# Two chunks of attention scores to a PSUM bank, and one mask matmul for both

## The chip, the cores and the metric

The kernel runs on one core of one Trainium2 chip. The metric is the device time of one execution in microseconds (us), lower is better. A time given for a kernel is the median of its runs; the profile is one execution of its own, taken by the hardware profiler.

## What is computed

Causal attention with a bias from a running sum, and behind it two feed-forward stages. The change lies in the attention alone (B = 4, H = 8, S = 576, D = 64):

```python
scores = scale * np.matmul(q, k.transpose(0, 1, 3, 2))
causal = np.triu(np.ones((S, S), dtype=bool), k=1)
cum = np.cumsum(np.maximum(s, 0.0), axis=-1)
bias = -(cum[:, :, :, None] - cum[:, :, None, :])
scores = np.where(causal, -1000000000.0, scores + np.minimum(bias, 0.0))
attn = np.exp(scores - np.max(scores, axis=-1, keepdims=True))
attn = attn / (np.sum(attn, axis=-1, keepdims=True) + 1e-09)
out = np.matmul(attn, v)
...
h = x @ w_in; g = h - np.tanh(h); x = g @ w_out        # 2304 x 512, width 2048
# then: each token through one of 8 experts, picked by argmax, width 1024
```

## The kernel before

**Tiling.** Two heads at a time fill the 128 partitions, which gives 16 pairs of heads, called heads below where no harm is done. The 576 queries of a pair are cut into nine chunks of 64; chunk c needs the first 64c + 64 keys. `score(c)` (lines 216 to 235) multiplies chunk c with those keys into a tile `sc`, one PSUM bank of 128 x 512 floats. It takes three matmuls on line 228, since each operand is split into a high and a low part. A fourth matmul (line 230) adds the causal mask to the last 64 columns: it multiplies the identity `identb` with `maskm`, a 128 x 64 block in bf16. Chunk 8 has 576 keys and takes two banks. One VectorE operation (line 233, called the reduction below) then adds the bias that waits in `P`, scales, writes the result to `P` and leaves the least value of each row in `m`. `expo(c)` (line 238) takes the exponential on ScalarE, with `m` as its bias and the sum of each row to `den`.

**What follows.** `ptr(g)` (line 253) transposes four blocks of `P` at a time into a tile `tp`; its copy to SBUF (line 135) is on VectorE for groups 0, 2 and 4 and on ScalarE for the others. `pv` (line 272) multiplies with V, and line 280 scales the result by the inverse of `den`, which makes a trip through DRAM in between (lines 292 to 323). GpSimd writes the bias (line 209) and makes the low parts of K and Q (line 181), from copies that ScalarE casts (lines 190 and 198). Beside this the weights of the next stage are converted on ScalarE and VectorE (lines 382 to 386).

**PSUM.** The eight banks are given out as rings: three for `tp`, four for `sc`, one for `pv`. A pair asks for ten `sc` banks. A bank is free again when its reduction is done.

**Order.** Each step has a place in time, a number in the table `AT`; pair number i adds 9 i to it, so that one unit is one chunk. The steps are written out in the order of these numbers. For pair i, `score(8 - n)` stands at n and its `expo` at n + 0.8; group 5 of the transposes at 5.5, group 3 at 6.5, group 4 at 7.5, group 1 at 8.5; the cast of a later pair's K falls at 8.5 as well. TensorE runs exactly in this order (`ORD[MA]`). The other engines are ordered by a planner, which starts from the same sequence and may move an instruction whose inputs are there earlier; `behind()` ties some steps, among them the conversion of weights on VectorE, to the last reduction written out before them (`k.mark["D"]`), or on ScalarE to the last exponential (`k.mark["A"]`).

Of the kernel before, what the change touches and what calls it, by code (L numbers as in the profile page):

```python
# [8 lines left out]
F32 = mybir.dt.float32  # L9
# [4 lines left out]
ALU = mybir.AluOpType  # L14
PSUM = bass.MemoryType.PSUM

B, H, S, D = 4, 8, 576, 64
# [21 lines left out]
def setup_attention(ctx, tc, k, s):  # L39
# [47 lines left out]

    k.qb = [[k.e1.tile([128, NCH, 128], F32R, name=f"qb{i}_{t}", tag=f"qb{i}_{t}", bufs=1) for t in range(2)] for i in range(NQB)]
    for i, q in enumerate(k.qb):
# [8 lines left out]
    for p in k.P:  # L98
# [4 lines left out]
NCH = 9  # L103
PW = [0, 128, 256, 512, 768, 1152, 1536, 2048, 2560, 3200]

BLK = [(kc, c) for kc in range(5) for c in range(2 * kc, NCH)]
NQB = 3

EV = {0: 'D', 1: 'A', 2: 'D', 3: 'A', 4: 'D', 5: 'A', 6: 'A'}
PIN = 'D1'  # L110
# [4 lines left out]
AT = {'ni': 14, 'no': 2, 'pad': 60.5, 'const': 42.5, 'wl': 6.2, 'cr': -9.0, 'load': -20.0, 'v': 6.0, 'ks': -9.5, 'qs': -8.5,  # L115
# [22 lines left out]
def attention_events(tc, k, q, kk, v, xT, b, hp, idx):  # L138

    nc = tc.nc  # L140
    bh = b * H + 2 * hp
    ld, wk, ps = k.ld, k.wk, k.psum
    ev = []
    T = {}
    P = k.P[idx % 2]
    qh, ql = k.qb[idx % NQB]

    def at(t):
        def deco(f):
            ev.append((9 * idx + t, f))  # L150
            return f
        return deco
# [48 lines left out]
    def chunk(c, lo=0, hi=None):  # L201
        return P[:, PW[c] + lo:PW[c] + (64 * c + 64 if hi is None else hi)]

    def bias(c):

        w = 64 * c + 64
        ci = k.cumi[:, c, bh // 2:bh // 2 + 1]
        if BIAS[c] == "P" and (idx or c % 2):
            ins = nc.gpsimd.tensor_scalar(chunk(c), T["cr"][:, 0:w], 1.0, ci, ALU.mult, ALU.add)  # L209
            behind(tc, k, "P", ins)  # L210
            k.mark["P"] = ins.ins.name
        else:
            nc.vector.tensor_scalar(chunk(c), T["cr"][:, 0:w], ci, None, ALU.add)


    def score(c):
        if c == NCH - 1:
            T["m"] = wk.tile([128, NCH], F32, name="m", tag="m")
            T["m2"] = wk.tile([128, 1], F32, name="m2", tag="m2")
            T["den"] = wk.tile([128, NCH], F32, name="den", tag="den")  # L220
        w = 64 * c + 64
        least = 3.0e38
        cuts = [0, 288, 576] if w > 512 else [0, w]
        for lo, hi in zip(cuts, cuts[1:]):
            sc = ps.tile([128, 512], F32, name="sc", tag="sc")
            n = hi - lo
            for i, (a, x) in enumerate(((qh, "kh"), (qh, "kl"), (ql, "kh"))):
                nc.tensor.matmul(sc[:, 0:n], a[:, c, :], T[x][:, lo:hi], start=(i == 0), stop=(i == 2 and hi < w))  # L228
            if hi == w:
                nc.tensor.matmul(sc[:, n - 64:n], k.identb, k.maskm, start=False, stop=True)  # L230
            dst = chunk(c, lo, hi)
            m = T["m"][:, c:c + 1] if hi == w else T["m2"]
            k.mark["D"] = nc.vector.tensor_tensor_reduce(  # L233
                out=dst, in0=sc[:, 0:n], in1=dst, scale=-0.125, scalar=least, op0=ALU.add, op1=ALU.min, accum_out=m).ins.name
            least = m

    def expo(c):
        k.mark["A"] = nc.scalar.activation(  # L238
            chunk(c), chunk(c), AF.Exp, bias=T["m"][:, c:c + 1], scale=-1.0, accum_out=T["den"][:, c:c + 1]).ins.name

    for n in range(NCH):
        at(n + AT["bias"] - (4 if idx == 0 and n % 2 else 0))(lambda c=NCH - 1 - n: bias(c))
        at(n)(lambda c=NCH - 1 - n: score(c))
        at(n + AT["exp"])(lambda c=NCH - 1 - n: expo(c))


    def ptr(g):
# [731 lines left out]
def tile_kernel(ctx, tc, q, kk, v, s, w_in, w_out, w_gate, w_og, w1, w2, out, dbg=None):  # L979
# [7 lines left out]
    with ExitStack() as abctx:  # L987
# [3 lines left out]
        with ExitStack() as actx:  # L991
# [14 lines left out]
            for i in range(16):  # L1006
                ev += attention_events(tc, k, q, kk, v, xT, i // 4, i % 4, i)
# [81 lines left out]
```

## Time and profile before

| | |
|---|---|
| median of 3 runs | 945.45 us |
| lowest and highest run | 936.3 and 946.69 us |
| the profiled execution | 940.23 us, its span 938.6 us |
| granted TensorE clock, mean of the span | 0.990 |
| busy, share of the span | PE 95%, PEld 81%, DVE 66%, ACT 57%, POOL 39% |
| attention | about the first 200 us of the span |

PE is TensorE's matmuls, PEld its weight loads (they overlap), DVE is VectorE, ACT ScalarE, POOL GpSimd, SP SyncE. Ends of matmuls are modelled and overlap the next one, so a matmul's cost is read from its start to the start of the next one, not from its length. An execution's own time is 1.6 us above its span.

### The profile page before, as it was taken

What the parts mean: (1) busy time and instruction counts of PE and PEld (TensorE: products, weight loads), DVE (VectorE), ACT (ScalarE), POOL (GpSimd) and SP (SyncE); (2) the same over time, 40 slices, a digit from 0 to 9 for tenths busy, and PEclk for the clock granted to TensorE, in tenths of its full rate; (3) what the DMA queues carried; (4) which work ended last, traced back from release to release, by engine and by line L of the source; (5) the groups of instructions that cost most, each with busy time, mean ns of one, the idle gap of its engine ahead of it and who ended that gap; (6) DMA issues with size and microseconds to landing.
All of it is one profiled execution on the core that took longest, in us unless ns stands there. A gap on an engine that the chain in (4) does not pass through costs nothing.

```text
span 938.6 us, 16275 instructions
## 1 busy us (share of the span) xinstructions
PE 895.0 (95%) x5840; PEld 764.0 (81%) x5841; DVE 618.3 (66%) x1343; ACT 536.2 (57%) x1092; POOL 361.5 (39%) x396
## 2 busy tenths in 40 slices
PE   7999999988999989999999999999899999999995
PEld 5777777767887778888989898988788888888884
DVE  7888888959898887786555555577535444445420
ACT  6888888846666558455555555566344444444421
POOL 8888888714444432333323232323221220220111
PEclk9999999989999999999999999999989999999998
DMA  6666666581221121000000000232565555564100
GB/s 207 187 196 202 201 202 199 171 274 46 68 68 47 66 68 64 5 1 24 1 23 1 23 1 24 84 121 88 132 226 166 179 163 166 164 191 142 50 24 29
DMA packets 41362, 100.82 MB, mean 107 GB/s; under 512 B 9313, under 2 KB 9445, under 8 KB 41277
## 3 DMA queue, kind: packets, MB, share of 16 engines
q1 hardware_dynamic: 37117, 89.51, 31.1%
q0 software_dynamic: 4160, 10.23, 3.1%
q8 instruction: 47, 0.77, 0.4%
q14 instruction: 38, 0.31, 0.1%
HBM read 84.74 MB, written 15.79 MB: 107 GB/s over the span
## 4 chain that ended last, share of the span: by engine, by line
PE 64%; DVE 15%; issue 9%; ACT 6%; DMA 4%; POOL 1%; SPq 0%; DVEq 0%; POOLq 0%; ACTq 0%
PE h L577 14%; PE x L607 12%; PE y L844 11%; PE hc L820 10%; PE sc L228 6%; PE pv L272 4%; PE tp L253 4%; DVE d L589 3%; DVE t L591 3%; DVE d L587 2%; DVE wt L385 1%; DVE wt L386 1%; ACT u L584 1%; ACT t L586 1%; ACT P L238 1%
## 5 line engine op out<-in xcount | busy, mean ns | idle before, releaser
L577 PE MATMUL h<-x_h,wi 128*128 128x256 f32 x1152 | 221.4, 285 | 3.3 <-DVE t L590 3.3
L594 POOL TENSOR_TENSOR gl<-t,gh 128x512 fp32r<-128x512 f32 x72 | 100.4, 1394 | 262.9 <-ACT gh L593 176.1
L577 PEld LDWEIGHTS h<-x_h,wi 128*128 128x128 f32 x1152 | 183.8, 191 | 11.2 <-PE x L607 6.4
L607 PE MATMUL x<-wo,gh 128*128 128x512 f32 x576 | 180.0, 393 | 0.3 <-POOL wo L525 0.3
L577 PE MATMUL h<-x_l,wi 128*128 128x256 f32 x576 | 162.8, 283 | 0.0
L607 PE MATMUL x<-wo,gl 128*128 128x512 f32 x288 | 115.0, 399 | 8.8 <-POOL gl L594 8.7
L587 DVE TENSOR_TENSOR d<-u,h 128x512 f32<-128x512 f32 x72 | 49.3, 685 | 105.7 <-ACT t L586 105.6
L607 PEld LDWEIGHTS x<-wo,gh 128*128 128x128 f32 x576 | 103.6, 189 | 18.7 <-POOL wo L525 0.7
L577 PEld LDWEIGHTS h<-x_l,wi 128*128 128x128 f32 x576 | 110.1, 191 | 1.3
L228 PE MATMUL sc<-kh,qb 128*128 128x288 f32 (+8 forms) x320 | 101.6, 347 | 0.7 <-DVE m L233 0.7
L238 ACT ACTIVATE P<-P,m 128x576 f32<-128x576 f32 (+2 forms) x144 | 81.2, 565 | 31.5 <-DVE m L233 30.5
L807 DVE SCALAR_TENSOR_TENSOR gl<-hc,gh 128x336 fp32r<-128x336 f32 (+2 forms) x66 | 32.8, 497 | 91.7 <-ACT gh L806 91.7
L593 ACT CAST gh<-t 128x512 fp32r<-128x512 f32 x72 | 44.7, 621 | 83.9 <-DVE t L591 60.9
L806 ACT ACTIVATE gh<-hc 128x336 fp32r<-128x336 f32 (+2 forms) x66 | 29.2, 443 | 95.8 <-PE hc L820 83.9
L820 PE MATMUL hc<-xgh,w_h 128*128 128x336 f32 (+1 forms) x256 | 82.1, 321 | 0.0
L742 DVE TENSOR_TENSOR w_l<-w_r,w_h 128x1024 fp32r<-128x1024 f32 (+1 forms) x72 | 79.5, 1113 | 3.1 <-PE h L577 2.7
L820 PE MATMUL hc<-xgh,w_l 128*128 128x336 f32 (+1 forms) x256 | 79.9, 312 | 0.0
L820 PE MATMUL hc<-xgl,w_h 128*128 128x336 f32 (+1 forms) x256 | 79.7, 311 | 0.0
L209 POOL TENSOR_SCALAR P<-cr,cumi 128x448 f32<-128x448 f32 (+4 forms) x139 | 78.1, 579 | 1.9 <-ACT cr L135 0.4
L607 PEld LDWEIGHTS x<-wo,gl 128*128 128x128 f32 x288 | 54.1, 188 | 28.0 <-POOL gl L594 16.7
L844 PE MATMUL y<-w_h,gh 128*128 128x512 f32 (+1 forms) x192 | 76.1, 397 | 0.0
L844 PE MATMUL y<-w_l,gh 128*128 128x512 f32 (+1 forms) x192 | 76.0, 396 | 0.0
(192 smaller groups left out, 1962.4 us busy)
## 6 DMA issues: line engine op xcount, KB each, us to landing
w_r<-in_moe_w_dram SPq DMA_DIRECT2D x64, 512.0 KB, 3.6
f64raw<-in_moe_w_in_dram SPq DMA_DIRECT2D x16, 512.0 KB, 4.4
f64raw<-in_moe_w_out_dram SPq DMA_DIRECT2D x16, 512.0 KB, 4.1
vt<-in_v_dram SPq DMA_DIRECT2D x16, 320.0 KB, 5.1
xk<-in_k_dram SPq DMA_DIRECT2D x16, 288.0 KB, 2.8
xq<-in_q_dram SPq DMA_DIRECT2D x16, 288.0 KB, 3.4
x_d<-x2s SPq DMA_DIRECT2D x9, 512.0 KB, 2.8
cr<-cum_d SPq DMA_DIRECT2D x30, 144.0 KB, 4.4
```

The costliest lines, as they stand in the source:

```text
L209: ins = nc.gpsimd.tensor_scalar(chunk(c), T["cr"][:, 0:w], 1.0, ci, ALU.mult, ALU.add)
L228: nc.tensor.matmul(sc[:, 0:n], a[:, c, :], T[x][:, lo:hi], start=(i == 0), stop=(i == 2 and hi < w))
L238: k.mark["A"] = nc.scalar.activation(chunk(c), chunk(c), AF.Exp, bias=T["m"][:, c:c + 1], scale=-1.0, accum_out=T["den"][:, c:c + 1]).ins.name
L253: nc.tensor.transpose(pt[:, 128 * i:128 * i + 128], chunk(c, 128 * kc, 128 * kc + 128), k.ident)
L577: nc.tensor.matmul(ps[:, i, :], a[f][:, c, :], x[:, c, :], start=(n == 0), stop=(n == 11))
L587: nc.vector.tensor_tensor(d, u, ps, ALU.mult)
L593: nc.scalar.copy(gh, t)
L594: k.mark["P"] = nc.gpsimd.tensor_tensor(gl, t, gh.bitcast(F32), ALU.subtract).ins.name
L607: nc.tensor.matmul(st["x2", g][t], a[:, i, 128 * t:128 * t + 128], w[f], start=(f == 0 and n == 0), stop=(f == 15 and n == 2),)
L742: pin(tc, "1D"[e > 0], nc.vector.tensor_tensor(l[:, a:z], r[:, a:z], h[:, a:z].bitcast(F32), ALU.subtract))
L820: nc.tensor.matmul(ps[:, 0:w], a[:, c, fo:fo + 128], x, start=(n == 0), stop=(n == 11))
L844: nc.tensor.matmul(st["y", e, c][0:n, :], a[:, o:o + n], w, start=(f == 0 and i == 0), stop=(f == 7 and i == 2),)
```

## The change

Chunk 2 is written into the bank of chunk 3, and chunk 0 into that of chunk 1 (`SECOND = (2, 0)`). The first chunk of each two starts the bank; the second is written behind it with no start flag, into columns that lie 64c + 128 in. The mask of the first chunk is left out. Once both are there, one matmul adds the mask to both: its output is two runs of 64 columns that lie apart, and its moving operand is `maskm` read twice. Then both reductions are issued, the earlier chunk first. So a pair asks for eight `sc` banks and has seven mask matmuls, where it had ten and nine. The reductions of chunks 3 and 1 are written out one unit later, and their exponentials 0.6 of a unit later. Chunks 8 to 4 are as before.

```diff
+SECOND = (2, 0)
...
-        least = 3.0e38
-        cuts = [0, 288, 576] if w > 512 else [0, w]
-        for lo, hi in zip(cuts, cuts[1:]):
-            sc = ps.tile([128, 512], F32, name="sc", tag="sc")
-            n = hi - lo
+        if w > 512:
+            cuts = [(0, 288, 0), (288, 576, 0)]
+        else:
+            cuts = [(0, w, 64 * c + 128 if c in SECOND else 0)]
+        for lo, hi, o in cuts:
+            two = c in SECOND or c - 1 in SECOND
+            if c not in SECOND:
+                T["sc"] = ps.tile([128, 512], F32, name="sc", tag="sc")
+            sc, n = T["sc"], hi - lo
             for i, (a, x) in enumerate(((qh, "kh"), (qh, "kl"), (ql, "kh"))):
-                nc.tensor.matmul(sc[:, 0:n], a[:, c, :], T[x][:, lo:hi], start=(i == 0), stop=(i == 2 and hi < w))
-            if hi == w:
+                nc.tensor.matmul(
+                    sc[:, o:o + n], a[:, c, :], T[x][:, lo:hi], start=(i == 0 and c not in SECOND), stop=(i == 2 and hi < w))
+            if c - 1 in SECOND:
+                continue
+            if c in SECOND:
+                d = sc[:, o - 64:o + n].rearrange("p (a j) -> p a j", j=64)
+                nc.tensor.matmul(
+                    d[:, 0::c + 1, :], k.identb, k.maskm.unsqueeze(1).broadcast_to((128, 2, 64)), start=False, stop=True)
+            elif hi == w:
                 nc.tensor.matmul(sc[:, n - 64:n], k.identb, k.maskm, start=False, stop=True)
-            dst = chunk(c, lo, hi)
-            m = T["m"][:, c:c + 1] if hi == w else T["m2"]
-            k.mark["D"] = nc.vector.tensor_tensor_reduce(
-                out=dst, in0=sc[:, 0:n], in1=dst, scale=-0.125, scalar=least, op0=ALU.add, op1=ALU.min, accum_out=m).ins.name
-            least = m
+            if c in SECOND:
+                least(c + 1, sc, 0, 0, w + 64, 3.0e38)
+            least(c, sc, o, lo, hi, 3.0e38 if lo == 0 else T["m2"])
+
+    def least(c, sc, o, lo, hi, start):
+        dst = chunk(c, lo, hi)
+        m = T["m"][:, c:c + 1] if hi == 64 * c + 64 else T["m2"]
+        k.mark["D"] = nc.vector.tensor_tensor_reduce(
+            out=dst, in0=sc[:, o:o + hi - lo], in1=dst, scale=-0.125, scalar=start, op0=ALU.add, op1=ALU.min, accum_out=m).ins.name
...
-        at(n + AT["exp"])(lambda c=NCH - 1 - n: expo(c))
+        at(n + AT["exp"] + (0.6 if NCH - 2 - n in SECOND else 0))(lambda c=NCH - 1 - n: expo(c))
```

## Rows read from the trace of the kernel before

**Rows 1.** Busy time by stretch: start:end, length, PE, PEld, DVE, ACT, POOL, clock, DMA.

```profile
90.00:120.00 30.00, 29.99 (x244) 23.40 (x243) 26.48 (x84) 23.81 (x67) 25.48 (x33) 1.00 0.67 197
...
0.00:200.00 200.00, 187.18 (x1492) 148.54 (x1493) 172.53 (x543) 158.65 (x443) 157.24 (x233) 1.00 0.66 198
```

**Rows 2.** Chain of work that ended last, 99.7 to 112 us: start, length, what.

```profile
by line: PE sc L228 43.5%; PE tp L253 28.7%; PE pv L272 24.5%; PE sc L230 3.3%; PE tp L298 0.9%
...
99.78 0.80 PE sc L228 x6
...
111.29 0.80 PE sc L228 x6
```

**Rows 3.** TensorE's matmuls in order of time, 105.7 to 110.7 us: start, length, what.

```profile
105.77 0.33 PE L228 MATMUL sc<-kh,qb 128*128 128x384 f32 x1
105.95 0.20 PE L230 MATMUL sc<-maskm,identb 128*128 128x64 bf16 x1
...
107.85 0.28 PE L228 MATMUL sc<-kh,qb 128*128 128x256 f32 x1
107.97 0.20 PE L230 MATMUL sc<-maskm,identb 128*128 128x64 bf16 x1
108.01 0.64 PE L253 MATMUL tp<-ident,P 128*128 128x128 f32 x4
...
108.80 0.20 PE L230 MATMUL sc<-maskm,identb 128*128 128x64 bf16 x1
...
109.55 0.28 PE L228 MATMUL sc<-kh,qb 128*128 128x128 f32 x1
109.67 0.21 PE L230 MATMUL sc<-maskm,identb 128*128 128x64 bf16 x1
...
110.44 0.21 PE L230 MATMUL sc<-maskm,identb 128*128 128x64 bf16 x1
110.63 0.66 PE L253 MATMUL tp<-ident,P 128*128 128x128 f32 x4
```

**Rows 4.** VectorE in order of time, 108.8 to 112 us; brackets hold the idle time before.

```profile
108.82 0.41 DVE L233 CUSTOM_DVE_ANT_0 P<-sc,P 128x256 f32<-128x256 f32 x1
...
109.16 0.35 DVE L233 CUSTOM_DVE_ANT_0 P<-sc,P 128x192 f32<-128x192 f32 x1
...
110.14 0.47 DVE L383 TENSOR_SCALAR wf<-wf 128x512 f32<-128x512 f32 x1 [0.63 <-ACT wf L382]
110.53 0.27 DVE L233 CUSTOM_DVE_ANT_0 P<-sc,P 128x128 f32<-128x128 f32 x1
...
110.73 0.60 DVE L384 TENSOR_SCALAR wf<-wf 128x512 int32<-128x512 int32 x1
111.26 0.67 DVE L135 COPY PT<-tp 128x512 f32<-128x512 f32 x1
111.85 0.21 DVE L233 CUSTOM_DVE_ANT_0 P<-sc,P 128x64 f32<-128x64 f32 x1
```

**Rows 5.** ScalarE in order of time, 110 to 113 us.

```profile
110.01 0.57 ACT L135 COPY PT<-tp 128x512 f32<-128x512 f32 x1
110.47 0.52 ACT L238 ACTIVATE P<-P,m 128x256 f32<-128x256 f32 x1
...
111.88 0.42 ACT L238 ACTIVATE P<-P,m 128x128 f32<-128x128 f32 x1
...
112.27 0.68 ACT L190 CAST kh<-xk 128x576 fp32r<-128x576 f32 x1
```

**Rows 6.** Waits, 20 to 230 us: who waited for whom, us in total, times, longest.

```profile
POOL kl L181 <- ACT kh L190: 20.0, 11, 2.7
...
DVE den L292 <- ACT P L238: 9.2, 13, 1.0
...
PEld sc L228 <- DVE m L233: 0.9, 1, 0.9
...
PE sc L228 <- DVE m L233: 0.7, 1, 0.7
```

## The prediction

> **What bounds the kernel now.** I read the busy time by stretch first, to see which stage the change can reach and who is full there. Attention takes the first 200 us or so of a 938.6 us span, and in a steady 30 us of it TensorE is busy for 29.99 us, VectorE for 26.48, GpSimd for 25.48 and ScalarE for 23.81, at the full granted clock [rows 1]. So TensorE has no gap, and the others have 10 to 20%. The chain of waits comes next: from 99.7 to 112 us it never leaves TensorE [rows 2]. The reader should see two things in it. One pair of heads takes 111.29 - 99.78 = 11.51 us, and the mask matmuls of line 230, all nine of them, hold 3.3% of that, about 0.4 us. That is the most that this change could ever find on TensorE if it took all masks away. Then come the start times on TensorE [rows 3], because ends are modelled, and the order on VectorE and ScalarE around chunks 3 to 0 [rows 4, 5], to see how long a reduction may be late before somebody waits. The whole change lies in 16 pairs; 1% of the kernel, 9.5 us, would be 0.59 us in each of them. I call 1% about what a measurement of this kernel can tell from no change, since three runs of the same kernel already lie 1.1% apart (936.3 to 946.69 us).
>
> **The masks taken away.** Two of nine mask matmuls go in each pair, 32 in all. A mask starts at 107.97 and the transposes behind it at 108.01 [rows 3]; nine times that is the 3.3% of the chain [rows 2]. The last score matmul ahead of it holds TensorE for 0.12 us whether a mask follows or not, I assume: with 128 columns and with 256 the step from it to the mask is 0.12 us both times (109.55 to 109.67, 107.85 to 107.97), which looks like a floor for such a matmul and not like something that the mask adds. So 32 x 0.04 = 1.3 us less.
>
> **The masks made wider.** The 32 that stay in the shared banks have 128 columns for 64. No row shows a bf16 matmul of 128 columns. Bounds: nothing more, if the 0.04 us is a floor of issue; or the 0.12 us of a score matmul with 128 columns [rows 3], which is 0.08 us more, 2.6 us in all. A slope lies between them: 384 columns take 105.95 - 105.77 = 0.18 us and 256 take 0.12 us, so 128 columns more cost 0.06 us and 64 more cost 0.03 us. The 64 columns that the mask has now would be 0.03 of its 0.04 us by that slope, so 128 would be about 0.06. I take 0.02 us more, since the slope is of the same engine and nearer than a matmul that loads a wider weight type: 32 x 0.02 = 0.6 us.
>
> The new mask also writes two runs of 64 columns that lie apart, and reads its moving operand twice. No matmul in this trace has such an output, so the trace leaves this open; I bound it from above by a matmul with four times the columns: 512 columns by the same slope cost 0.24 us, 0.20 more than the mask now, which is 6.4 us over 32. From below it is nothing, as the runs are long. I take nothing, since a run of 64 has few breaks, and keep the 6.4 us as a rival. The Trainium skill, page "PSUM — Partial Sum Buffer", section "Specifications (TRN2)", says that any access pattern that is not contiguous slows matmuls significantly. That speaks against this change; it gives no figure, and no row here can show it. By that rule rival (a) below would come true.
>
> **The score matmuls without a start flag** do the same work in other columns; nothing.
>
> **The reductions of chunks 3 and 1 come later.** They now wait for the mask of chunks 2 and 0. What stands behind them on VectorE is the other reduction, a conversion of weights and a copy of transposes; their readers are the exponentials on ScalarE. For chunk 3 the code has no VectorE step between its old place and its new one. The mask of chunk 2 starts 0.83 us after that of chunk 3 (107.97 to 108.80) [rows 3], and VectorE is so far behind that the reduction of chunk 3 starts only at 108.82 today [rows 4]. It would slip by about 0.2 us, the length of a mask. Its exponential starts at 110.47 [rows 5], behind a copy, so 1.2 us of slack hide it. For chunk 1 two steps lie in between, the copy of group 4 and a conversion on line 384, which no longer has a reduction of chunk 1 to queue behind. So I expect conversion, conversion, copy, and then the two reductions together. The reduction of chunk 1 then moves from 110.53 to 110.53 + 0.53 (line 384) + 0.59 (the copy) = 111.65, and that of chunk 0 to 111.65 + 0.20 = 111.85, where it is now [rows 4]. The exponential of chunk 1 stands at 111.88 and could start when that reduction has ended, at about 112.0 [rows 5]: 0.1 to 0.2 us late. Behind it on ScalarE stand the cast of K, which GpSimd waits for (up to 2.7 us at a time), and the exponential of chunk 0, for which VectorE's `den` step waits 9.2 us in 13 pairs [rows 6]. None of this is on TensorE's chain; GpSimd and VectorE have 15 and 12% of the stretch idle [rows 1], 1.3 us or more in a pair, and 0.2 us goes there. If that cover were gone, it would cost 16 x 0.2 = 3.2 us.
>
> **The exponentials moved by 0.6.** From 5.8 to 6.4 and from 7.8 to 8.4 no other ScalarE step lies in between (group 3 stands at 6.5, the cast of K at 8.5), so the queue of ScalarE keeps its order. They issue no DMA and pass none on ScalarE; SyncE's loads keep their places. Nothing.
>
> **Fewer banks.** Eight are asked for in a pair for ten, so a bank comes round later: the next pair's chunk 7, say, waits for the reduction of chunk 2 where it waited for that of chunk 1. TensorE waited for reductions 0.7 + 0.9 us in all the 20 to 230 us [rows 6]; 0 to 1.6 us less. I take 0, since these are single waits that may well be at the start or end of the stage.
>
> **The sum** is -1.3 + 0.6 = -0.7 us. One place may swallow part of it: behind the mask of chunk 0 the transposes start only 0.19 us later, not 0.04 [rows 3], and ScalarE's copy that frees their tile ends at 110.01 + 0.57 = 110.58 [rows 5]. So TensorE meets ScalarE there once in a pair, and what it gains up to there is waited for if ScalarE doesn't move too. The ends of the sum are -1.3 - 1.6 = -2.9 us, and with the wide mask at its bound and the slip uncovered -1.3 + 2.6 + 3.2 = +4.5 us. On the profiled execution of 940.23 us it makes 939.5 us. That execution lies 5.2 us below the median of the runs, which is more than all that is summed here; on the median it makes 945.45 - 0.7 = 944.8 us, my forecast.
>
> **Rivals.** (a) The split output is slow: 6.4 us for 32 masks less 1.3 saved is +5.1 us, 950.5 us. For it speaks that no such matmul has run here; against it, that the runs are long. Still within 1%. (b) Slower: the queue of VectorE. If the planner puts more ahead of the two late reductions than I listed, ScalarE, which takes its queue in order, stands still at the exponential of chunk 1, and with it the cast of K, GpSimd's low parts, and the copies that free the `tp` tiles for TensorE. That decides from the point where the reduction of chunk 1 is over 1.1 us late (it ends at 110.81 now, the exponential starts at 111.88 [rows 4, 5]) by more than the 1.3 us of idle time of VectorE. One further step of some 0.6 us a pair on TensorE's chain, as long as line 384 or the copy, is 16 x 0.6 = 9.6 us, less 0.7: 954.4 us, and up to 957 with the slip. Against it: by the code only the two steps named lie between. (c) It doesn't do what it says: TensorE gives up the time at its meeting with ScalarE, and nothing changes: 945.4 us. (d) Faster: all 2.9 us are had, 942.5 us. That is not 1%; for a figure of that size the runs themselves would have to fall low, as the 936.3 us of one run before did.
>
> **How the numbers follow.** Chances: the forecast 0.57, (a) 0.10, (b) 0.11, (c) 0.12, (d) 0.10. The forecast, (c) and (d) differ by less than the runs do, so their times spread as the runs before did: the range starts from the lowest run less most of the best end of the sum, 936.3 - 2.3 = 934, and reaches up to the highest run with (a), 946.69 + 5.1 = 951.8, say 952, which leaves out most of (b). Faster by over 1% means below 936.0 us, which takes a median at the low run: 0.12, from the forecast and (d). Slower by over 1% means above 954.9 us: 0.09, from (b) and little of (a). The rest, 0.79, is within 1%.
>
> **What would show it.** In the changed profile line 230's successor has 112 mask matmuls for 144; the wide ones should hand over to the next matmul after 0.05 to 0.07 us, and after 0.2 or more by (a). The period of a pair should be 11.45 to 11.5 us, the chain in the middle of attention still TensorE's alone; by (b) it would run over VectorE and ScalarE, with the period above 12 us. The reduction of chunk 1 should stand right ahead of that of chunk 0, its exponential no more than 0.2 us later, against the mask of chunk 0, than now. What would make me wrong: the planner orders the other engines anew in stages that I take as untouched, or the clock falls in a wait at the end of attention that isn't there now.

## The result and the profile after

| | before | after |
|---|---|---|
| median of 6 runs each | 939.06 us (935.8 to 946.69) | 929.09 us (928.27 to 929.99) |
| ratio | | 0.9881, 95% interval 0.985 to 0.9913 |
| the profiled execution, its span | 940.23, 938.6 us | 928.81, 927.1 us |
| start of the last score matmul | 192.52 us | 185.95 us |
| from there to the first matmul of the next stage | 16.07 us | 11.58 us |
| from there to the end | 729.97 us | 729.61 us |

The change makes the kernel 1.2% faster by the ratio, 10 us by the medians, where the forecast was 0.7 us. The forecast of 944.8 us missed by 15.7 us: 6.4 of these are the base (the median of before was 945.45 us from three runs when it was made, and is 939.06 us here with three more), 9.3 us are the effect beyond the 0.7 us that were forecast. In the profiled executions 6.6 us went in the pairs of heads, 4.5 us in the stretch right behind them, and 0.4 us in all the rest.

The busy time of the changed kernel looks as that of before did: the page, then a steady stretch by windows (same columns as in [rows 1]).

```profile
PE 884.7 (95%) x5808; PEld 757.2 (82%) x5809; DVE 613.5 (66%) x1343; ACT 537.9 (58%) x1092; POOL 367.4 (40%) x396
```

```profile
100.00:130.00 30.00, 30.00 (x255) 24.35 (x252) 26.23 (x88) 26.32 (x74) 27.05 (x34) 1.00 0.71 211
```

TensorE is as full as in [rows 1], 30.00 of 30 us, and yet a pair now takes 11.01 us for 11.5. A figure of busy time that doesn't move while the work in it gets done 4% sooner wasn't the bound that it seemed to be. The chain of waits of the changed kernel, one pair (start, length, what):

```profile
107.60 0.07 PE sc L243
107.67 0.44 PE tp L273 x4
...
108.91 0.04 PE sc L246
108.95 0.47 PE tp L273 x4
...
117.10 0.07 PE sc L243
117.17 0.44 PE tp L273 x4
```

And pieces of the same chain before, from the stretch of [rows 2] but not shown there:

```profile
100.62 0.57 PE tp L253 x4
...
108.17 0.47 PE tp L253 x4
...
109.00 0.54 PE tp L253 x4
...
110.65 0.64 PE tp L253 x4
```

Here the reader is to see the first fact: before, four equal transposes take 0.47 us in one place and 0.57, 0.54 and 0.64 us in others. After, each four take 0.44 to 0.47. The work is the same, so the excess of 0.10 + 0.07 + 0.17 = 0.34 us in a pair was waiting. It shows as busy time because a matmul's end is modelled. This explains 0.34 of the 0.5 us that a pair gained; most of the rest, 0.12 us, is the masks (below).

The wide mask of chunks 1 and 0 itself, in TensorE's order of time:

```profile
118.45 0.23 PE L243 MATMUL sc<-maskm,identb 128*128 128x128 bf16 x1
118.52 0.61 PE L273 MATMUL tp<-ident,P 128*128 128x128 f32 x4
```

It hands over after 0.07 us; the one of chunks 3 and 2 in the same pair after 0.06 us.

**Where the waiting went.** The code was changed around chunks 3 to 0, but the planner also moved other steps. In a steady pair VectorE's queue before was: chunk 8's first half, `den` (line 292), chunk 8's second half, reciprocal, a copy of transposes, the fifth and last step of the weight conversion (line 386, *the step* below), chunk 7, `xT`. After, it is: first half, copy, second half, `den` (line 312), the step (line 406), reciprocal, chunk 7, `xT`. VectorE and GpSimd of before over that stretch (start, length, engine, line, operation, output <- input):

```profile
113.81 0.67 DVE L292 TENSOR_SCALAR den<-den 128x9 f32<-128x9 f32 x1 [0.76 <-ACT P L238]
...
115.50 1.39 DVE L386 SCALAR_TENSOR_TENSOR wf<-f64raw,wf 128x512 int32<-128x512 int32 x1
116.81 0.68 DVE L233 CUSTOM_DVE_ANT_0 P<-sc,P 128x512 f32<-128x512 f32 x1
```

```profile
113.03 1.42 POOL L181 TENSOR_TENSOR kl<-xk,kh 128x576 fp32r<-128x576 f32 x1 [1.98 <-ACT kh L190]
114.42 0.54 POOL L209 TENSOR_SCALAR P<-cr,cumi 128x320 f32<-128x320 f32 x1
114.92 3.26 POOL L181 TENSOR_TENSOR qb<-xq,qb 64x576 fp32r<-64x576 f32 x2
```

The same two engines after:

```profile
122.44 0.54 DVE L312 TENSOR_SCALAR den<-den 128x9 f32<-128x9 f32 x1
122.90 0.68 DVE L406 SCALAR_TENSOR_TENSOR wf<-f64raw,wf 128x512 int32<-128x512 int32 x1
...
123.62 0.62 DVE L254 CUSTOM_DVE_ANT_0 P<-sc,P 128x512 f32<-128x512 f32 x1
```

```profile
121.54 1.42 POOL L183 TENSOR_TENSOR kl<-xk,kh 128x576 fp32r<-128x576 f32 x1 [1.53 <-ACT kh L192]
122.93 1.05 POOL L211 TENSOR_SCALAR P<-cr,cumi 128x320 f32<-128x320 f32 x1
123.95 2.93 POOL L183 TENSOR_TENSOR qb<-xq,qb 64x576 fp32r<-64x576 f32 x2
```

The same operation on the same shape takes 1.39 us before and 0.68 us after. Before, it starts 0.58 us after GpSimd has begun the first of the two low parts of Q, 1.42 us long; that ends at 116.34, and the step ends 0.55 us later. After, the step stands right behind `den`, starts as the low part of K ends, and runs at once; now GpSimd's bias is the one that takes 1.05 us in place of 0.54. In these rows whichever of the two starts first is served, and the other stands still until it has ended. The Trainium skill, page "SBUF — State Buffer", section "Who interferes with whom", says that a VectorE instruction with two inputs in SBUF contends with a GpSimd instruction that reads SBUF, and that the order of issue decides who blocks. The rows agree, in both directions: 0.71 us lost by VectorE before, 0.51 us by GpSimd after. On VectorE the reductions and the copies that free `tp` stand behind the step; GpSimd has 1.53 us of idle time ahead of its low part of K in the same fence, which covers its own loss.

ScalarE shows the next link: its exponential of chunk 7 waits for the reduction that stands behind the step. Before, then after:

```profile
117.54 0.72 ACT L238 ACTIVATE P<-P,m 128x512 f32<-128x512 f32 x1 [1.61 <-DVE m L233]
```

```profile
124.29 0.72 ACT L258 ACTIVATE P<-P,m 128x512 f32<-128x512 f32 x1 [0.34 <-DVE m L254]
```

In the kernel before this wait is 1.48 to 1.66 us in each of the 13 pairs in which the step is held, and 0.35 us at most in the other three. The copies that free `tp` on ScalarE stand behind it.

The kernel before holds the contrast within itself: in the pair that begins at 30.89 us the step wins (34.71 to 35.39 us, 0.68 us long), in the next one and all later steady ones it loses (46.20 to 47.59 us and so on). The pairs that begin at 30.89 and 42.05 us take 11.16 and 11.18 us, and from 53.23 us on a pair takes 11.49 us or more. So the pair in which the step first loses is not yet longer; the loss shows from the next one on.

### The profile page after: what moved, and what is told of

It is laid out like the page before. It is cut to its first block, busy times and chain, and to the rows that moved or that the text cites. A ratio compares the mean times of both kernels' runs of the same rounds, so it can differ in the third digit from the quotient of the medians.

```text
span 927.1 us, 16181 instructions
## 1 busy us (share of the span) xinstructions
PE 884.7 (95%) x5808; PEld 757.2 (82%) x5809; DVE 613.5 (66%) x1343; ACT 537.9 (58%) x1092; POOL 367.4 (40%) x396
## 3 DMA queue, kind: packets, MB, share of 16 engines
q0 software_dynamic: 4160, 10.23, 3.2%
## 4 chain that ended last, share of the span: by engine, by line
PE 62%; DVE 14%; issue 9%; ACT 5%; POOL 4%; DMA 4%; SPq 1%; DVEq 0%; POOLq 0%; ACTq 0%
PE h L597 14%; PE x L627 12%; PE y L864 12%; PE hc L840 10%; PE sc L236 4%; PE pv L292 3%; DVE d L609 3%; PE tp L273 3%; DVE t L611 3%; POOL P L211 2%; DVE d L607 2%; DVE wt L405 1%; DVE wt L406 1%; DMA rdb<-rden_d 1%; ACT u L604 1%
## 5 line engine op out<-in xcount | busy, mean ns | idle before, releaser
L211 POOL TENSOR_SCALAR P<-cr,cumi 128x448 f32<-128x448 f32 (+4 forms) x139 | 88.1, 650 | 1.9 <-ACT cr L137 0.4
```

## The experiments

My first theory was another one: that the period hangs on VectorE's `den`, which stands still for an exponential of ScalarE ([rows 6], 9.2 us in 13 pairs) and was moved behind chunk 8's second half by the change. The rival was that ScalarE's new order, copies of transposes ahead of exponentials, does it. Experiment 1 asks for the masks, 2 to 7 for these two theories, both of which fell, and 8 for the stretch behind the last score. The median of before was 936.96 us beside 1 to 4, 938.61 beside 5 to 8 and 939.98 beside 9 to 12; a ratio is taken over all the runs and need not equal the quotient of two medians.

**1. Each chunk its own mask, in the shared banks** (an edit of the kernel after).

```diff
+            if c in SECOND or c - 1 in SECOND:
+                nc.tensor.matmul(sc[:, o + n - 64:o + n], k.identb, k.maskm, start=False, stop=c in SECOND)
...
             if c in SECOND:
-                d = sc[:, o - 64:o + n].rearrange("p (a j) -> p a j", j=64)
-                nc.tensor.matmul(d[:, 0::c + 1, :], k.identb, k.maskm.unsqueeze(1).broadcast_to((128, 2, 64)), start=False, stop=True)
+                pass
```

> The changed kernel with one thing undone: each chunk has a mask matmul of its own again, 144 in all, still in the shared banks; the other engines' orders are those of the changed kernel. Theory (the gain comes from the order of VectorE and ScalarE, which no longer make a loop of 11.5 us a pair): the period stays near 11.05 us, the time within 2 us of the changed kernel's 929.09, so 928 to 931 us. Rival (the gain comes from the mask matmuls that are gone): the time goes back to that of the kernel before, 936 to 946 us, with a period near 11.5 us.

Measured: 928.75 us, ratio 0.9894 (0.9839 to 0.995), period 11.13 us for 11.01. So the masks are worth 0.12 us in a pair, 1.9 us in 16, and that is not to be told apart in the time. The one matmul for both masks isn't what made most of the gain.

**2. ScalarE's old order in the kernel after.**

```diff
...
-        at(n + AT["exp"] + (0.6 if NCH - 2 - n in SECOND else 0))(lambda c=NCH - 1 - n: expo(c))
+        at(n + AT["exp"] + {3: 0.6, 2: -0.35, 1: 0.6}.get(NCH - 1 - n, 0))(lambda c=NCH - 1 - n: expo(c))
...
+        if g in (3, 1):
+            behind(tc, k, "A", ins)        # the copy of transposes, as before
```

> The changed kernel with ScalarE's old order: the copy of transposes of group 3 behind the exponentials of chunks 3 and 2, that of group 1 behind the cast of K. VectorE's order stays the changed one, with the den step behind the second reduction of chunk 8. Theory (a loop through the den step): one old half does not close the loop, so the period stays at 11.0 to 11.15 us and the time within 3 us of 929. Rival (TensorE simply waits for ScalarE's copies to free its transposes' banks): 0.3 to 0.4 us a pair come back, the period is near 11.4 us and the time 934 to 937 us.

Measured: 927.57 us, 0.9883 (0.9826 to 0.9941), period 11.01 us. ScalarE's new order isn't needed.

**3. `den` ahead of chunk 8's second half in the kernel after**, as it was before.

```diff
...
+        if lo and idx:
+            k.mark["D"] = k.den
+            behind(tc, k, "D", ins)
...
```

> The changed kernel with the den step put ahead of the second reduction of chunk 8 on VectorE, as it was before; ScalarE's order stays the changed one. Theory: as long as the copy of group 1 does not stand ahead of the last exponential, den waits less than 0.4 us and the period stays at 11.0 to 11.2 us, 929 to 932 us. Rival (the den step's place alone): period 11.4 us or more, 934 us or more.

Measured: 928.74 us, 0.9909 (0.9844 to 0.9975), period 11.01 us. The new place of `den` isn't needed either.

**4. Both old orders in the kernel after** (the edits of 2 and 3, and the copy of group 2 put behind the reciprocal). Banks and masks stay as changed.

> The changed kernel, shared banks and joint masks and all, with the old order on both engines: den and the second reduction of chunk 8 ahead of the copy of group 2 on VectorE, and the copies behind exponentials and cast on ScalarE. Theory: the loop is closed again, VectorE waits 0.7 us at den in most pairs, the period is 11.4 to 11.6 us and the time 934 to 941 us. Rival (masks and banks): the period stays near 11.0 us, 928 to 931 us.

Measured: 939.24 us, 1.0012 (0.9948 to 1.0076), period 11.78 us. The whole gain is gone, with every mask and bank of the change in place. (A pair is even 0.28 us longer than before; that surplus wasn't looked into.) In this kernel the step stands behind the copy again, and GpSimd is ahead of it:

```profile
117.16 1.40 DVE L416 SCALAR_TENSOR_TENSOR wf<-f64raw,wf 128x512 int32<-128x512 int32 x1
```

```profile
116.59 3.25 POOL L183 TENSOR_TENSOR qb<-xq,qb 64x576 fp32r<-64x576 f32 x2
```

**5. `den` behind the second half in the kernel before**, one line.

```diff
-        nc.vector.tensor_scalar(den, den, 1.0e-9, None, ALU.add)
+        behind(tc, k, "D", nc.vector.tensor_scalar(den, den, 1.0e-9, None, ALU.add))
```

> The kernel before with one edge: the den step is queued on VectorE behind the second reduction of the next pair's chunk 8. Nothing else, all 144 masks and ten banks as before. Theory (the loop through den sets the pair's period): the 0.5 us of that reduction leave the loop, so the period falls from 11.5 to between 11.0 and 11.25 us and the time to 929 to 935 us. Rival (the changed kernel is faster for something in its banks or its PE work): no change, 936 to 946 us, period 11.5.

Measured: 936.4 us, 0.9964 (0.9922 to 1.0007). The theory fell here: `den` waits for no exponential any more, and a pair still takes 11.5 us from the fifth one on.

```profile
89.81 0.68 DVE L292 TENSOR_SCALAR den<-den 128x9 f32<-128x9 f32 x1
...
91.11 1.77 DVE L386 SCALAR_TENSOR_TENSOR wf<-f64raw,wf 128x512 int32<-128x512 int32 x1
92.81 0.68 DVE L233 CUSTOM_DVE_ANT_0 P<-sc,P 128x512 f32<-128x512 f32 x1
```

```profile
90.93 3.24 POOL L181 TENSOR_TENSOR qb<-xq,qb 64x576 fp32r<-64x576 f32 x2
```

What the trace shows in place of the wait is a step of 1.77 us, which starts 0.18 us after GpSimd's low part of Q. All that `den` gained the step lost: chunk 7 starts 2.36 us behind the end of GpSimd's low part of K (90.45 us), as it does in the kernel before (114.45 to 116.81 us). This row led to the theory that stands now.

**6. ScalarE's new order in the kernel before**, own banks and own masks.

```diff
...
-        at(n + AT["exp"])(lambda c=NCH - 1 - n: expo(c))
+        at(n + AT["exp"] + {3: 0.75, 1: 0.75}.get(NCH - 1 - n, 0))(lambda c=NCH - 1 - n: expo(c))
...
+        if g in (3, 1):
+            k.mark["A"] = ins.ins.name     # exponentials 3 and 1 queue behind the copies
```

> The kernel before, its own banks and masks, with ScalarE's copies of groups 3 and 1 queued ahead of the exponentials of chunks 3 and 1, about as in the changed kernel; the planner then also puts den behind the second reduction of chunk 8. Theory: the loop is open, the period is 11.1 to 11.2 us (0.1 above the changed kernel's for the two extra masks), the time 928 to 934 us, as fast as the changed kernel. Rival (banks and masks): 936 to 946 us.

Measured: 930.07 us, 0.9892 (0.983 to 0.9954), period 11.13 us. As fast as the change with no mask or bank touched. It would speak for ScalarE's order if 2 didn't speak against it; but the planner answered this edit on VectorE too: the step stands behind `den` and ahead of the reciprocal, and takes 0.68 us in the steady pairs.

**7. Only the late reductions and exponentials in the kernel before**, own banks and masks.

```diff
+            if c - 1 in SECOND:
+                T["sc"] = sc
+                continue
+            if c in SECOND:
+                least(c + 1, T["sc"], 0, w + 64, 3.0e38)
...
```

> The kernel before with the late reductions and late exponentials of the change alone: chunk 3 is reduced together with chunk 2, chunk 1 with chunk 0, but each chunk has its own bank and its own mask. The planner, free to reduce chunk 1 early, keeps ScalarE's old order and keeps den ahead of the second reduction of chunk 8. Theory: the loop stays closed, the period 11.4 to 11.8 us, the time 935 to 946 us. Rival (the late reductions themselves help): period near 11.1 and 928 to 932 us.

Measured: 937.14 us, 0.9999 (0.9959 to 1.0038), period 11.5 us. The step is still behind the copy and takes 1.40 us. So the lateness alone isn't it: with own banks the planner doesn't come to the other order from it.

**8. The weight casts behind the last copy of `rt` on ScalarE**, in the kernel before, for the stretch behind the last score.

```diff
...
+            k.mark["A"] = ins.ins.name     # ins is the copy to rt of the last pair
```

> The kernel before with one edge at the end of attention: on ScalarE the casts of the next stage's weights, which wait for a DMA, are queued behind the copy of the last pair's inverse sums. Theory for the 4.5 us that the changed kernel saves between the last scores and the first matmul of the next stage: TensorE stood still for 3 us because this copy waited behind those casts, and ran the next 5 us at a lower clock for it; so that stretch falls from 16.1 to 11 to 12.5 us and the median by 2 to 5 us, with the period still 11.5 us. Rival (an accident of one profile): the stretch is short anyway and the time within 1 us of the kernel before.

Measured: 937.15 us, 0.9989 (0.9956 to 1.0022); the stretch took 11.83 us for 16.07, and the time didn't move. In the profiles of 4, 5 and 7, without this edit, it took 10.89, 10.95 and 11.24 us, and in that of 9, with the same wait as before, 16.21 us. So the long stretch is there in some profiled executions and not in others; no run shows that the change takes it away.

The last four test the theory of the blocked step.

**9. The step one place later in the kernel before**, behind chunk 7: one number.

```diff
-      'n2': 13.0, 'w0': 5.4, 'wt': (0, 1.2, 2.2, 3.2, 4.2), 'ws': 6.0, 'wd': 9, 'wr': 8}
+      'n2': 13.0, 'w0': 5.4, 'wt': (0, 1.2, 2.2, 3.2, 4.8), 'ws': 6.0, 'wd': 9, 'wr': 8}
```

> The kernel before with one number changed: the last integer step of the weight conversion stands one place later on VectorE, behind the reduction of chunk 7 (den, chunk 8's second half, reciprocal, copy, chunk 7, step) and not ahead of it. Own banks, own masks and ScalarE's order as before. Theory (the step is held until GpSimd's first low part of Q has ended, 1.40 us in place of 0.68, and chunk 7's reduction stands behind it): chunk 7's reduction comes 0.7 to 1.3 us earlier, the step still waits but with less behind it, period of a pair 11.0 to 11.2 us in place of 11.5, time 929 to 933 us. Rival (what pays is that VectorE's den and conversion, or ScalarE's copies, stand earlier): nothing stands earlier here, period stays 11.5, 936 to 939 us.

Measured: 952.97 us, 1.0135 (1.0078 to 1.0192), slower than both forecasts.

```profile
108.01 0.68 DVE L233 CUSTOM_DVE_ANT_0 P<-sc,P 128x512 f32<-128x512 f32 x1
...
108.62 0.80 DVE L386 SCALAR_TENSOR_TENSOR wf<-f64raw,wf 128x512 int32<-128x512 int32 x1
110.96 0.56 DVE L280 TENSOR_TENSOR xT<-pv,rdb 128x192 f32<-128x192 f32 x2 [1.53 <-DMA rdb<-rden_d]
```

The local part came as expected: GpSimd's low part of K ends at 106.96 here and at 114.45 before, so chunk 7 starts 1.05 us behind it for 2.36, which is 1.3 us earlier, and the step takes 0.80 us. But the next wait, which I had left out, took more than that: `xT` waits 1.53 us for the reciprocals' transfers. The chain of waits of that kernel:

```profile
101.79 5.10 DMA rden_d<-rt
```

The step's result is stored by a DMA (line 1022) that stands in SyncE's queue just ahead of the reciprocals' first transfer, with a load of 512 KB between them, and the planner had put another transfer ahead of the three as well, the load of `cr` (line 176):

```profile
100.15 0.45 SPq L176 DMA_DIRECT2D cr<-cum_d  x1
...
101.79 0.36 SPq L305 DMA_DIRECT2D rden_d<-rt  x1
```

It is this load and not the step that held the queue: the step of that pair had ended at 97.21 us, and `cr` was issued when GpSimd's last bias from the old `cr` had ended, at 100.12 us. The reciprocals lay ready in `rt` at 97.68 us, and their transfer was issued 4.1 us later; before it is 1.1 us (118.50 to 119.59 us). This run doesn't decide between the theories; it shows that moving the step moved SyncE's queue too.

**10. The step right behind `den` in the kernel before**, all masks and banks and ScalarE's order as before; `den` and the step ahead of chunk 8's second half.

```diff
-      'bias': -4.0, 'exp': 0.8, 'n0': 9.2, 'n1': 11.55,
+      'bias': -4.0, 'exp': 0.8, 'n0': 8.85, 'n1': 11.55,
-      'n2': 13.0, 'w0': 5.4, 'wt': (0, 1.2, 2.2, 3.2, 4.2), 'ws': 6.0, 'wd': 9, 'wr': 8}
+      'n2': 13.0, 'w0': 5.4, 'wt': (0, 1.2, 2.2, 3.2, 3.55), 'ws': 6.0, 'wd': 9, 'wr': 8}
...
+            if lo and idx:
+                k.mark["D"] = k.w4         # chunk 8's second half queues behind the step
+                behind(tc, k, "D", ins)
...
+                if n == 4:
+                    k.mark["D"] = k.den    # the step queues behind den
...
```

> The kernel before with the same step moved the other way, right behind den (chunk 8's first half, den, step, reciprocal, chunk 8's second half, copy, chunk 7); all else as before. Theory: den is itself held until GpSimd's low part of K ends, so the step that stands right behind it gets in ahead of GpSimd's bias and takes 0.68 us; the bias then takes about 1.05 in place of 0.53; period 11.0 to 11.2, 929 to 933 us. Rival (ScalarE's copies set the period): 11.5, 936 to 939 us. If the step still shows 1.4 us in the old place's manner, the theory's account of who gets in first is wrong.

Measured: 929.91 us, 0.9885 (0.9835 to 0.9935), period 11.13 us.

```profile
110.19 0.68 DVE L296 TENSOR_SCALAR den<-den 128x9 f32<-128x9 f32 x1 [0.45 <-ACT P L242]
110.79 0.68 DVE L390 SCALAR_TENSOR_TENSOR wf<-f64raw,wf 128x512 int32<-128x512 int32 x1
```

```profile
109.42 1.43 POOL L181 TENSOR_TENSOR kl<-xk,kh 128x576 fp32r<-128x576 f32 x1 [0.94 <-ACT kh L190]
110.83 1.04 POOL L209 TENSOR_SCALAR P<-cr,cumi 128x320 f32<-128x320 f32 x1
```

```profile
106.90 0.47 PE tp L257 x4
...
107.67 0.47 PE tp L257 x4
```

Each number is the one that was expected: the step 0.68 us, the bias 1.04, the period 11.13. `den` still waits for the exponential (0.45 us), ScalarE has its old order, and each four transposes of this chain take 0.47 us (last fence, two of them): the 0.34 us of waiting are gone.

**11. GpSimd's low part of Q in six shorter instructions** in the kernel before; VectorE's order unchanged.

```diff
-            low(LO[1 + h], ql[p, :, o], x, qh[p, :, o])
+            for a, z in ((0, 3), (3, 6), (6, 9)):
+                low(LO[1 + h], ql[p, a:z, o], x[:, a:z], qh[p, a:z, o])
```

> The kernel before with the same order on every engine; only GpSimd's low part of Q is written by six instructions of three chunks each in place of two of nine. Theory: what holds the step is one instruction of GpSimd, 1.41 us long; with a third of that length the step takes at most about 1.1 us, the period falls to 11.1 to 11.35, and the time to 930 to 935 us (GpSimd's fixed cost of four more instructions in a pair, by the 0.53 us of its bias of 320 columns at most 0.3 us each, may take part of it back). Rival (the period is set elsewhere): 11.5 or more, 936 to 941 us.

Measured: 937.98 us, 0.9981 (0.9946 to 1.0015).

```profile
104.55 1.13 DVE L387 SCALAR_TENSOR_TENSOR wf<-f64raw,wf 128x512 int32<-128x512 int32 x1
```

```profile
103.97 3.92 POOL L181 TENSOR_TENSOR qb<-xq,qb 64x192 fp32r<-64x192 f32 x6
```

The step takes 1.13 us for 1.39 with no order changed, so what holds it is the GpSimd instruction that is under way. Five of the pairs take 11.25 or 11.26 us, as expected, but between them stand pairs of 11.54 to 13.05 us. In the chain of waits these lie on the reciprocals' transfers, of which the first takes 3.98 us in a pair of 11.9 us and 6.69 us in the next, of 13.05 us:

```profile
109.30 3.98 DMA rden_d<-rt
...
120.54 6.69 DMA rden_d<-rt
```

The expected time failed. The expected period held where the first of these transfers landed early: at most 2.0 us behind the pair's start in the five pairs, 4.0 us behind it in the one of 13.05 us.

**12. A version beyond both: the pads' DMAs apart.** One pair of the kernel after takes 13.02 us. Its chain of waits, in part:

```profile
84.77 0.34 SPq L417
...
87.34 4.24 DMA rdb<-rden_d
```

SyncE's queue stood still for a memset on GpSimd (line 416, done just ahead of the first row), with the reciprocals' transfers behind it, the last of which lands at 91.58 us. The edit issues the two DMAs 11 units later, a little over a period.

```diff
...
             ev.append((AT["pad"], lambda: pads(tc, k)))
+            ev.append((AT["pad"] + 11, lambda: pads_out(tc, k)))   # the two DMAs
```

> The kernel after with one more edit: the two DMAs that write the pads to DRAM are issued a period behind the memsets that they wait for, so that the DMA queue of SyncE doesn't stand still ahead of the transfers of the reciprocals. Theory: the one pair that took 13.02 us takes 11.0 to 11.1, 926.5 to 928 us against 929.1 for the change. Rival (SyncE's queue is late there for another reason): 13.0 stays, 929 us.

Measured: 927.39 us, 0.9855 (0.9805 to 0.9905); the pair takes 11.01 us. The last score matmul starts at 184.76 us for 185.95: 2.0 us were gained in that pair and 1.2 given back in the first one (10.23 us for 9.07), beside smaller ones. Against the change the gain is 1.7 us by the medians. The intervals of the two ratios overlap, so it isn't told apart from none, though five of its six runs lie below all six of the change.

**All of them at once.** Over the twelve kernels and the two given ones, a step of 0.62 to 0.70 us in the steady pairs goes with a period of 11.01 to 11.13 us and 927 to 930 us (after, 1, 2, 3, 6, 10, 12). A step of 1.4 to 1.8 us goes with 11.5 to 11.8 us and 936 to 940 us (before, 4, 5, 7, 8). Cases 9 and 11 lie between for the step and lost their time to the reciprocals' transfers. A single held step can stay free: one of 1.52 us in experiment 3 stands among pairs of 11.01 us.

## Why the prediction was wrong, point by point

**The masks: right mechanism, both terms mis-sized.** 0.12 us in a pair (experiments 1 and 10 against the kernels with joint masks: 11.13 against 11.01), 1.9 us in 16, for a forecast of 0.7 us and a bound of 2.9. The wide mask hands over after 0.06 to 0.07 us, as forecast, but the four transposes behind it are shorter by as much: 0.07 + 0.44 us for 0.04 + 0.47 behind a narrow one, both in the chain of the changed kernel. So the widening, put at 0.6 us, cost nothing, and a mask that is gone gave 0.06 us where 0.04 was forecast. Rival (a) is out: the split output cost nothing that shows. The Trainium skill, page "PSUM — Partial Sum Buffer", section "Specifications (TRN2)", would have it slow significantly; for two runs of 64 columns the measured 0.03 us more than a mask of 64 columns doesn't bear that out.

**"So TensorE has no gap": the step that failed.** From 29.99 busy us in 30 and a chain that never left TensorE I took it that only work taken from TensorE can shorten a pair, and put its waiting at nothing. The runs show 0.34 us of waiting in a pair of 11.5 us. Experiment 10 takes it away with every mask and bank of before in place; in experiment 4 the whole gain is gone with every mask and bank of the change in place. The chain had the contradiction in it, four equal transposes at 0.47 and at 0.64 us, and pairs of 11.16 us beside pairs of 11.5 us in the same kernel. I saw the long step behind chunk 0's mask ([rows 3], 0.19 us) and booked it as a place that swallows gain, not as a wait that could go.

**"None of this is on TensorE's chain; GpSimd and VectorE have 15 and 12% of the stretch idle ..., and 0.2 us goes there": wrong in kind.** A share of idle time said nothing of two engines that stop each other. The order that I worked out for the late reductions was right (conversion, conversion, copy, then both reductions), and their slip was larger than forecast. ScalarE after:

```profile
120.40 0.41 ACT L258 ACTIVATE P<-P,m 128x128 f32<-128x128 f32 x1 [0.61 <-DVE m L254]
```

Chunk 1's exponential starts 120.40 - 118.45 = 1.95 us behind the mask of chunk 0, where it was 111.88 - 110.44 = 1.44 us [rows 3, 5]: 0.5 us late, for at most 0.2 forecast. It cost nothing that shows. And VectorE, said to be "so far behind" at chunk 3 that the late mask would hardly matter, now stands still 1.05 us for it (to 117.31 us). Rival (b), built on that slip, didn't come.

**"The exponentials moved by 0.6 ... Nothing": wrong.** ScalarE's order did change, the copies of groups 3 and 1 moved ahead of the exponentials of chunks 3 and 1, though by experiment 2 this has no price.

**What I named as what would make me wrong** is what came, "the planner orders the other engines anew", though I gave it no chance and no price. The step's move to right behind `den` lies in no edited line.

**What stays open.** How the time held on VectorE reaches TensorE is read from traces (the reduction of chunk 7 and ScalarE's wait for it, copies behind them, `tp` tiles freed later) and was not tried link by link; nor was the reverse of experiment 10, the kernel after with the step alone put back behind the copy. Nor do the pairs account for the whole 10 us. Between 7 and 10, which differ in VectorE's order around the step and in the late reductions, both accounts agree: the last score matmul starts at 193.14 and 186.13 us, 7.0 us apart, and the medians lie 7.2 us apart. For the 10 us of the change, 6.6 us are in the pairs; the 4.5 us behind them are of one profiled execution. What the pairs leave goes in part with the mean granted clock that is listed for each run. Of the 49 runs of before in the batches, the ten at 0.993 or 0.994, where all six of the change lie, have a median of 936.9 us, 7.8 us above the change; the eleven at 0.985 or less took 940.8 to 950.3 us. By this, about 2 of the 10 us come with the lower clock of before's runs. One place of it is seen: in the stretch from 665 to 705 us of the kernel after (first fence) the mean granted clock is 0.91 and of experiment 5 (second fence) 0.74. As its two levels are 2.4 and 1.2 GHz, the lower one, half, held for (1 - 0.91) x 2 x 40 = 7 us and for 21 us. Experiments 4 and 8 show the long form too, 7, 10 and before's own profile the short one:

```profile
665.00:705.00 40.00, 34.20 (x209) 29.64 (x208) 13.49 (x20) 15.03 (x23) 11.90 (x12) 0.91 0.65 227
```

```profile
665.00:705.00 40.00, 36.25 (x181) 32.34 (x180) 11.99 (x17) 11.63 (x18) 10.08 (x10) 0.74 0.58 183
```

Why it falls for longer in some executions wasn't tried.

## What to carry to other kernels

Before a stage is called bound by TensorE, compare equal groups of matmuls within the chain: where the same four transposes took 0.47 us in one place and 0.64 in another, the difference was a wait, whatever the busy share said; and compare equal pairs with each other. Look for an operation whose time on the same shape differs (0.68 and 1.39 us) and lay the other engine's instruction beside it. A change that moves any due time in a planned kernel is a change of every queue that the planner fills, so compare the orders first, and judge the change's own idea by a kernel in which the old orders are put back.

## What the runs showed of the hardware that I had not expected

VectorE's step with two inputs in SBUF (128 x 512, int32) took 0.68 us where it started first, 1.39 to 1.40 us where a GpSimd subtraction of 1.42 us had begun 0.57 or 0.58 us earlier, 1.77 us where it had begun 0.18 us earlier, and 1.13 us where that subtraction was cut in three. In each case of an uncut one it ended about 0.55 us after GpSimd's instruction. `den`, 128 x 9 numbers, took 0.67 us beside the reciprocal's 0.20 us on the same shape, and ended when GpSimd's low part of K ended, before and in experiment 10.

The stretch behind the last score showed the price of a short wait of TensorE: before, the copy of `rt` stood behind a weight cast that waited for its transfer, TensorE waited 3.0 us for that copy, the granted clock was at half, the level of 1.2 GHz, from 199.5 to 206.3 us, and the same matmuls took 2.18 and 4.92 us where they take 1.26 and 2.88 us after. The chain before, then after:

```profile
200.03 2.18 PE sc L316 x36
202.21 4.92 PE pv L272 x28
```

```profile
191.92 1.26 PE sc L336 x36
193.18 2.88 PE pv L292 x28
```

```profile
199.50:206.30 6.80, 6.27 (x58) 4.21 (x60) 2.22 (x5) 2.31 (x6) 2.90 (x2) 0.50 1.02 359
```

The last fence is the window of before in which the clock was at half. Experiment 9 shows it again: after the same wait the 36 matmuls of the first group take 2.19 us.
